# Weight rounding in a top-k attention kernel: the sign bit made on GpSimd, and the first piece loaded in halves

## The chip, the cores and the metric

The kernel runs on one core of a Trainium2 chip. The metric is the time of one execution on the device, in microseconds. Before the change it is 1476.7 us (median of three runs, 1475.35 to 1476.87); the profiled execution spans 1473.8 us.

## The reference

```python
# attention: q, k, v are (8, 8, 576, 64); top_k = 32
scores = scale * np.matmul(q, k.transpose(0, 1, 3, 2))
kth = np.partition(scores, -top_k, axis=-1)[..., -top_k:-top_k + 1]
mask = scores >= kth
scores = np.where(mask, scores, -1000000000.0)
scores = scores - np.max(scores, axis=-1, keepdims=True)
attn = np.exp(scores)
attn = attn / (np.sum(attn, axis=-1, keepdims=True) + 1e-09)
attn_out = np.matmul(attn, v)
# MLP on the heads laid side by side: x is (4608, 512)
h = x @ w_in                      # w_in (512, 2048)
g = np.maximum(0.01 * h, h)
out = (g @ w_out)                 # w_out (2048, 512)
```

The two weight matrices are float64 in the inputs (a float32 array divided or multiplied by a double scale), and the kernel gets them as 16-bit words, four to a number. Before it can use them it has to round each number to float32 on the chip. That rounding is all the change is about.

## The kernel before

The weights come in sixteen pieces of 128 x 1024 numbers, 1 MB each as 16-bit words. Word 3 of each number holds the sign, the exponent and the top four bits of the mantissa; word 2 and words 0 and 1 hold the rest. The piece is taken apart on three engines, TensorE adds three scaled parts up in PSUM, and VectorE multiplies the sum by a power of two with the sign in it.

```python
    raws = ctx.enter_context(tc.tile_pool(name="raws", bufs=3))
    work = ctx.enter_context(tc.tile_pool(name="work", bufs=2))
    ...
    def load_weights(n):
        ...
        raw_of[n] = raws.tile([P, WCH, 4], U16, name="raw")
        nc.sync.dma_start(raw_of[n].rearrange("p n w -> p (n w)"), weights[n])   # L102

    def round_weights(n):
        raw = raw_of.pop(n)
        dst = piece(n)
        mid = raw[:, :, 2]
        low = raw.rearrange("p n w -> p (n w)").bitcast(U32).rearrange("p (n w) -> p n w", w=2)[:, :, 0]
        top = raws.tile([P, WCH], U16, name="top", bufs=2)
        scale = raws.tile([P, WCH], U16, name="scale", bufs=2)
        parts = work.tile([P, 2 * NKC - 1, P], F32, name="wT", bufs=3)
        ...                                             # m_top, m_low lie in parts
        nc.gpsimd.tensor_copy(top, raw[:, :, 3])                                  # L119
        nc.scalar.activation(dst, mid, AF.Copy, bias=-7.0 - 2.0 ** -16, scale=2.0 ** -20)   # L120
        nc.scalar.activation(m_low, low, AF.Copy, bias=128.0, scale=2.0 ** -29)   # L122
        yield
        nc.vector.tensor_scalar(scale, top, 4, 0x7FF, ALU.logical_shift_right, ALU.bitwise_and)   # L124
        nc.vector.tensor_scalar(scale, scale, 1151.0, 896.0, ALU.min, ALU.max)    # L126
        if n < NPIECE - 2:
            nc.scalar.activation(scale, scale, AF.Copy, bias=-896.0 * 128, scale=128.0)   # L128
        else:
            nc.vector.tensor_scalar(scale, scale, 896.0, 128.0, ALU.subtract, ALU.mult)   # L130
        nc.vector.tensor_scalar(m_top, top, 0xF, 0x3F80, ALU.bitwise_and, ALU.bitwise_or)  # L131
        nc.vector.tensor_scalar(top, top, 0x8000, None, ALU.bitwise_and)          # L132
        ...                                             # pw: a PSUM tile
        for pw, c in sums:                              # two halves of 512
            at = slice(c, c + 512)
            nc.tensor.matmul(pw, ident_top, m_top[:, at].bitcast(BF16), start=True, stop=False)   # L142
            nc.tensor.matmul(pw, ident, dst[:, at], start=False, stop=False)      # L143
            nc.tensor.matmul(pw, ident_low, m_low[:, at], start=False, stop=True) # L144
        yield
        nc.vector.tensor_tensor(scale, scale, top, ALU.bitwise_or)                # L146
        for pw, c in ends:
            at = slice(c, c + pw.shape[-1])
            nc.vector.tensor_tensor(dst[:, at], pw, scale[:, at].bitcast(BF16), ALU.mult)   # L149
```

The three sections between the yields belong to three steps. At step n the kernel issues the first section of piece n, the second of piece n - 1 and the third of piece n - 2, and then the load of piece n + 3:

```python
        for n in range(3):
            load_weights(n)
        for n in range(NPIECE + 2):
            for i in (n, n - 1, n - 2) if AS_WORDS else ():
                if 0 <= i < NPIECE:
                    if i == n:
                        rounding[i] = round_weights(i)
                    next(rounding[i], None)
            load_weights(n + 3)
            ...                                         # first loads of q, k, v; first scores
```

After it comes the attention, in 144 units of 128 rows of two heads, with the MLP's matmuls laid between its steps. Of it the text needs the first instruction of the top-k search and the mask:

```python
    def top_k(u):
        ...
        for n, op in enumerate((ALU.max, ALU.min)):
            nc.vector.tensor_tensor(pairs[:, :, n, :], u.both[:, :, 0:HS], u.both[:, :, HS:S], op)   # L244
        ...                                             # rounds of max (L249) and match_replace (L252)

    def mask(u, i):
        if i == 0:
            ...
            nc.gpsimd.tensor_scalar(u.nbias, u.tops[:, :, 0, 0], -SCALE, None, ALU.mult)          # L260
        pen = work.tile([P, S], F32, name="pen", bufs=1)
        nc.gpsimd.tensor_scalar(pen, u.s[i], u.tops[:, i, ROUNDS - 1, 7:8], MASKED, ALU.is_lt, ALU.mult)   # L262
        nc.gpsimd.tensor_tensor(u.s[i], u.s[i], pen, ALU.add)                     # L263

    def transpose(u):
        ...
            split = work.tile([P, 2 * S], U16, name="split", bufs=2)
            nc.scalar.copy(split, pairs[:, :, h])                                 # L287
```

Of the kernel before, what the change touches and what calls it, by code (L numbers as in the profile page):

```python
# [10 lines left out]
U16 = mybir.dt.uint16  # L11
BF16 = mybir.dt.bfloat16
AF = mybir.ActivationFunctionType
ALU = mybir.AluOpType
# [5 lines left out]
def kernel(  # L20
# [13 lines left out]
    nc = tc.nc  # L34
    NPAIR, P, S = qT.shape
# [14 lines left out]
    WCH = 1024  # L50
# [11 lines left out]
    work = ctx.enter_context(tc.tile_pool(name="work", bufs=2))  # L62
# [22 lines left out]
    def piece(n):  # L85

        if n < NPIECE // 2:
            j, c = divmod(n, HP)
            return w_in[c][:, j * WCH:(j + 1) * WCH]
        f = 2 * (n - NPIECE // 2)  # L90
        return w_out[f // 4][:, f % 4:f % 4 + 2, :].rearrange("p g n -> p (g n)")

    raw_of = {}

    def load_weights(n):
        if n >= NPIECE:
            return
        if not AS_WORDS:
            nc.sync.dma_start(piece(n), weights[n])
            return  # L100
        raw_of[n] = raws.tile([P, WCH, 4], U16, name="raw")
        nc.sync.dma_start(raw_of[n].rearrange("p n w -> p (n w)"), weights[n])  # L102

    def round_weights(n):

# [10 lines that stand above are left out]
        parts = work.tile([P, 2 * NKC - 1, P], F32, name="wT", bufs=3)  # L116
        parts = parts.rearrange("p c n -> p (c n)").bitcast(U16)
        m_top, m_low = parts[:, 0:WCH], parts[:, WCH:2 * WCH].bitcast(BF16)
        nc.gpsimd.tensor_copy(top, raw[:, :, 3])  # L119
        nc.scalar.activation(dst, mid, AF.Copy, bias=-7.0 - 2.0 ** -16, scale=2.0 ** -20)  # L120

        nc.scalar.activation(m_low, low, AF.Copy, bias=128.0, scale=2.0 ** -29)  # L122
        yield
        nc.vector.tensor_scalar(scale, top, 4, 0x7FF, ALU.logical_shift_right, ALU.bitwise_and)  # L124

        nc.vector.tensor_scalar(scale, scale, 1151.0, 896.0, ALU.min, ALU.max)  # L126
        if n < NPIECE - 2:
            nc.scalar.activation(scale, scale, AF.Copy, bias=-896.0 * 128, scale=128.0)  # L128
        else:
            nc.vector.tensor_scalar(scale, scale, 896.0, 128.0, ALU.subtract, ALU.mult)  # L130
        nc.vector.tensor_scalar(m_top, top, 0xF, 0x3F80, ALU.bitwise_and, ALU.bitwise_or)  # L131
        nc.vector.tensor_scalar(top, top, 0x8000, None, ALU.bitwise_and)  # L132
        if n < NPIECE - 4 or n % 2 == 0:
            tag, bufs = ("wide", 2) if n < NPIECE - 4 else ("narrow", 1)
            pw = ps_sc.tile([P, 2, 512], F32, name=tag, bufs=bufs)
            sums = [(pw[:, h, :], h * 512) for h in range(2)]
            ends = [(pw.rearrange("p h n -> p (h n)"), 0)]
        else:
            ends = sums = [(ps_ml.tile([P, 512], F32, name="pw", tag="ml"), h * 512) for h in range(2)]
        for pw, c in sums:  # L140
            at = slice(c, c + 512)
            nc.tensor.matmul(pw, ident_top, m_top[:, at].bitcast(BF16), start=True, stop=False)  # L142
            nc.tensor.matmul(pw, ident, dst[:, at], start=False, stop=False)  # L143
            nc.tensor.matmul(pw, ident_low, m_low[:, at], start=False, stop=True)  # L144
        yield
        nc.vector.tensor_tensor(scale, scale, top, ALU.bitwise_or)  # L146
        for pw, c in ends:
            at = slice(c, c + pw.shape[-1])
            nc.vector.tensor_tensor(dst[:, at], pw, scale[:, at].bitcast(BF16), ALU.mult)  # L149
# [319 lines left out]
    with tc.manual_schedule():  # L469
# [11 lines left out]
        for n in range(3):  # L481
            load_weights(n)
        rounding = {}
# [7 lines that stand above are left out]
            if 6 <= n < 6 + HP:  # L491
                load_qk(n - 6)
            elif n == NPIECE - 3:
                first_scores(steps[0])
            elif n == NPIECE:
                first_scores(steps[1])
            if n == NPIECE - 1:
                load_v(0)
                load_v(1)
# [132 lines left out]
```

## Time and profile before

| | busy us | share of the span |
|---|---|---|
| TensorE matmuls (PE) | 1393.5 | 95% |
| VectorE (DVE) | 1328.3 | 90% |
| GpSimd (POOL) | 1097.7 | 74% |
| ScalarE (ACT) | 1096.2 | 74% |

| instruction of the rounding | engine | count | mean us |
|---|---|---|---|
| L119 copy of word 3 | GpSimd | 16 | 1.14 |
| L120, L122 conversions | ScalarE | 16 each | 1.15, 1.13 |
| L124, L126, L131, L132 on 16-bit words | VectorE | 16 each | 0.43, 0.43, 0.42, 0.43 |
| L146, both inputs 16-bit | VectorE | 16 | 0.68 |
| L149, 1024 numbers at once | VectorE | 14 | 1.22 |

In the lines of the profile, L is a line of the kernel, then come the engine, the operation, and what is written, an arrow, and what is read. In lists of groups, what follows the bar is the busy time of the group in us and the mean of one in ns, and behind the next bar the idle time before it with what ended it. In the timeline and in the chain the first number is the start in us from the beginning of the span and the second the duration; a line that ends in x2 is two instructions merged.

### The profile page before, as it was taken

The numbers are of one execution on the slowest core, as the hardware profiler recorded it, in microseconds if no ns is written. First come the engines' busy times: TensorE is split into PE (matmuls) and PEld (weight loads), VectorE is DVE, ScalarE is ACT, GpSimd is POOL, SyncE is SP. The second block draws the span as 40 slices with busy tenths as digits, with TensorE's granted clock in tenths as the row PEclk, the third lists the DMA queues.
The fourth block names the chain that finished last, engine by engine and source line by source line (L and its number), as shares of the span: only waits on it lengthen the run. The fifth ranks groups of instructions, "written<-read, shape, count | busy, mean of one in ns | idle before, by whom it ended". The sixth has DMA issues, their size and how long they took to land.

```text
span 1473.8 us, 24093 instructions
## 1 busy us (share of the span) xinstructions
PE 1393.5 (95%) x8057; PEld 927.6 (63%) x8059; DVE 1328.3 (90%) x3414; ACT 1096.2 (74%) x1979; POOL 1097.7 (74%) x742
## 2 busy tenths in 40 slices
PE   6716989999999999999999999999999999999998
PEld 2304547676766666666666666767676767676674
DVE  7999999999999999999999999999999999999600
ACT  8647887777787777777777777787877787877710
POOL 2278887888788888788878887888788888787700
PEclk9957999999999999999999999999999999999999
DMA  9724453655367554666466545565557555554510
GB/s 331 298 64 127 131 153 102 175 157 148 105 166 206 142 146 129 180 181 150 135 167 189 155 125 147 165 196 142 130 165 207 138 141 132 165 135 135 144 47 14
DMA packets 391421, 223.48 MB, mean 152 GB/s; under 512 B 336256, under 2 KB 336257, under 8 KB 389249
## 3 DMA queue, kind: packets, MB, share of 16 engines
q1 hardware_dynamic: 391296, 221.95, 53.6%
q8 instruction: 63, 1.03, 0.3%
q14 instruction: 62, 0.50, 0.1%
HBM read 46.14 MB, written 92.60 MB: 94 GB/s over the span
## 4 chain that ended last, share of the span: by engine, by line
PE 81%; DVE 14%; DMA 2%; ACT 2%; issue 1%; SPq 0%; POOL 0%; DVEq 0%; ACTq 0%
PE pz L390 31%; PE ph L378 30%; PE wide L327 10%; PE wide L214 6%; DVE tops L249 5%; DVE pairs L252 4%; PE narrow L214 3%; DVE pairs L244 1%; DMA wT<-apart 1%; ACT split L287 1%; DVE w_out L149 1%; DVE w_in L149 1%; DVE scale L146 1%; DVE scale L124 0%; ACT s_sb L278 0%
## 5 line engine op out<-in xcount | busy, mean ns | idle before, releaser
L262 POOL TENSOR_SCALAR pen<-s_sb,tops 128x576 f32<-128x576 f32 x288 | 638.3, 2216 | 207.7 <-DVE tops L249 120.2
L249 DVE MAX8 tops<-pairs 128x8 f32<-128x288 f32 (+1 forms) x1152 | 635.9, 591 | 0.0
L390 PE MATMUL pz<-w_out,gT 128*128 128x512 f32 x1152 | 508.4, 596 | 0.0
L378 PE MATMUL ph<-x,w_in 128*128 128x256 f32 x2176 | 481.1, 381 | 0.0
L252 DVE MATCH_REPLACE8 pairs<-tops,pairs 128x288 f32<-128x288 f32 (+1 forms) x864 | 460.1, 538 | 0.0
L378 PEld LDWEIGHTS ph<-x,w_in 128*128 128x128 f32 x2176 | 410.7, 190 | 77.1 <-issue 22.9
L263 POOL TENSOR_TENSOR s_sb<-s_sb,pen 128x576 f32<-128x576 f32 x288 | 406.9, 1413 | 24.0
L390 PEld LDWEIGHTS pz<-w_out,gT 128*128 128x128 f32 x1152 | 215.3, 190 | 265.8 <-issue 264.8
L287 ACT COPY split<-s_sb 128x1152 uint16<-128x1152 uint16 x282 | 309.1, 1145 | 0.0
L278 ACT ACTIVATE s_sb<-s_sb,rz 128x576 f32<-128x576 f32 x288 | 207.0, 769 | 38.7 <-DVE rz L275 38.5
L266 ACT ACTIVATE s_sb<-s_sb,nbias 128x576 f32<-128x576 f32 x288 | 221.0, 767 | 12.5 <-POOL s_sb L263 12.5
L244 DVE TENSOR_TENSOR pairs<-s_sb 128x576 f32<-128x576 f32 x288 | 213.6, 780 | 9.9
L327 PEld LDWEIGHTS wide<-wT,vt 128*64 128x64 f32 x3200 | 161.7, 139 | 67.4 <-ACT s_sb L221 26.5
L327 PE MATMUL wide<-wT,vt 128*64 128x128 f32 (+1 forms) x3200 | 179.9, 269 | 24.6 <-ACT s_sb L221 22.3
L384 ACT ACTIVATE gT<-ph 128x512 f32<-128x512 f32 x136 | 80.6, 593 | 80.0 <-PE ph L378 80.0
L341 ACT COPY x<-wide 128x128 f32<-128x128 f32 (+1 forms) x160 | 32.1, 260 | 131.5 <-PE wide L327 131.4
L221 ACT COPY s_sb<-wide 128x704 f32<-128x704 f32 x142 | 107.0, 754 | 23.2 <-PE wide L214 23.1
L214 PE MATMUL wide<-kt,qt 64*128 64x352 f32 (+1 forms) x392 | 75.8, 500 | 26.0 <-ACT s_sb L221 23.6
L221 ACT COPY s_sb<-narrow 128x448 f32<-128x448 f32 x142 | 68.7, 536 | 1.3 <-PE narrow L214 0.7
L397 ACT COPY o_sb<-pz 128x512 f32<-128x512 f32 x36 | 21.1, 585 | 59.4 <-PE pz L390 59.4
L275 DVE RECIPROCAL rz<-ze 128x2 f32<-128x2 f32 x144 | 22.3, 155 | 44.8 <-ACT ze L271 44.7
L252 DVE MATCH_VALUE_LOAD pairs<-tops,pairs 128x8 f32 x864 | 62.5, 72 | 0.0
(62 smaller groups left out, 622.7 us busy)
## 6 DMA issues: line engine op xcount, KB each, us to landing
apart<-split SPq DMA_DIRECT2D x282, 288.0 KB, 2.1
raw<-in_weights_dram SPq DMA_DIRECT2D x16, 1024.0 KB, 6.9
vt<-in_vk_dram SPq DMA_DIRECT2D x32, 320.0 KB, 3.4
out_dram<-o_sb SPq DMA_DIRECT2D x36, 256.0 KB, 2.0
qt<-in_qT_dram SPq DMA_DIRECT2D x20, 288.0 KB, 3.2
kt<-in_kT_dram SPq DMA_DIRECT2D x20, 288.0 KB, 3.6
raw<-in_qT_dram SPq DMA_DIRECT2D x12, 288.0 KB, 3.2
raw<-in_kT_dram SPq DMA_DIRECT2D x12, 288.0 KB, 3.7
```

What stands on the lines that cost most here:

```text
L214: nc.tensor.matmul(to[r0:r0 + u.rows, i, :], qt[d, u.q0:u.q0 + u.rows], kt[d, k0:k1], start=True, stop=True)
L244: nc.vector.tensor_tensor(pairs[:, :, n, :], u.both[:, :, 0:HS], u.both[:, :, HS:S], op)
L249: nc.vector.max(out=u.tops[:, i, r, :], in_=rest[i])
L252: nc.vector.match_replace(out=rest[i], in_to_replace=u.tops[:, i, r, :], in_values=rest[i], imm_value=LOWEST)
L262: nc.gpsimd.tensor_scalar(pen, u.s[i], u.tops[:, i, ROUNDS - 1, 7:8], MASKED, ALU.is_lt, ALU.mult)
L263: nc.gpsimd.tensor_tensor(u.s[i], u.s[i], pen, ALU.add)
L266: nc.scalar.activation(u.s[i], u.s[i], AF.Exp, bias=u.nbias[:, i:i + 1], scale=SCALE, accum_out=u.z[:, i:i + 1])
L278: nc.scalar.activation(u.s[i], u.s[i], AF.Copy, bias=0.0, scale=u.rz[:, i:i + 1])
L287: nc.scalar.copy(split, pairs[:, :, h])
L327: nc.tensor.matmul(po[side * D:(side + 1) * D, o, :], vt[:, c, side, :], u.wT[:, c + side * NKC if c + 1 < NKC else c, r:r + n], start=(c ...
L378: nc.tensor.matmul(ph[:, i, 0:n], w_in[c][:, f * P:(f + 1) * P], x[c][:, 0:n], start=(c == 0), stop=(c == HP - 1),)
L390: nc.tensor.matmul(pz[0:m, 0:DMODEL], gT[:, f, r0:r0 + m], w_out[f // 4][:, f % 4, :], start=(f == 0), stop=(f == NFC - 1),)
```

## The change

The sign bit was made on VectorE from the copied word (L132, in place). Now GpSimd makes it straight from the loaded words: a word of 32768 or more has its top bit set, so the comparison gives 1 or 0, and the multiplication by 32768 puts the bit where it belongs. This takes one instruction from VectorE and gives one to GpSimd. The sign has a buffer of its own now, which it shares by name with the later "split" tiles (two of them). Beside that, piece 0 is loaded and taken apart in two halves of 512 numbers, so that its first half can be worked on before the second has landed; L124 and L126 follow in halves for that piece, the rest works on the whole.

```diff
+    def parts_of(n):
+
+        step = WCH // 2 if n == 0 else WCH
+        return [slice(c, c + step) for c in range(0, WCH, step)]
...
-        nc.sync.dma_start(raw_of[n].rearrange("p n w -> p (n w)"), weights[n])
+        for at in parts_of(n):
+            nc.sync.dma_start(raw_of[n].rearrange("p n w -> p (n w)")[:, 4 * at.start:4 * at.stop],
+                              weights[n][:, 4 * at.start:4 * at.stop])
...
-        nc.gpsimd.tensor_copy(top, raw[:, :, 3])
-        nc.scalar.activation(dst, mid, AF.Copy, bias=-7.0 - 2.0 ** -16, scale=2.0 ** -20)
-
-        nc.scalar.activation(m_low, low, AF.Copy, bias=128.0, scale=2.0 ** -29)
+        sign = work.tile([P, 2 * S], U16, name="split", bufs=2)[:, 0:WCH]
+        for at in parts_of(n):
+            nc.gpsimd.tensor_copy(top[:, at], raw[:, at, 3])
+            nc.scalar.activation(dst[:, at], mid[:, at], AF.Copy, bias=-7.0 - 2.0 ** -16, scale=2.0 ** -20)
+
+            nc.scalar.activation(m_low[:, at], low[:, at], AF.Copy, bias=128.0, scale=2.0 ** -29)
+        nc.gpsimd.tensor_scalar(sign, raw[:, :, 3], 32768.0, 32768.0, ALU.is_ge, ALU.mult)
         yield
-        nc.vector.tensor_scalar(scale, top, 4, 0x7FF, ALU.logical_shift_right, ALU.bitwise_and)
-
-        nc.vector.tensor_scalar(scale, scale, 1151.0, 896.0, ALU.min, ALU.max)
+        for at in parts_of(n):
+            nc.vector.tensor_scalar(scale[:, at], top[:, at], 4, 0x7FF, ALU.logical_shift_right, ALU.bitwise_and)
+
+            nc.vector.tensor_scalar(scale[:, at], scale[:, at], 1151.0, 896.0, ALU.min, ALU.max)
...
-        nc.vector.tensor_scalar(top, top, 0x8000, None, ALU.bitwise_and)
...
-        nc.vector.tensor_tensor(scale, scale, top, ALU.bitwise_or)
+        nc.vector.tensor_tensor(scale, scale, sign, ALU.bitwise_or)
```

## The prediction

> **What bounds the kernel now.** I read the page first, then the window sums, the chain of waits inside the first 70 us, the waits by engine, and last the timeline of the engines that the change touches. In the page's slices TensorE stands at 9 tenths or more from about a tenth of the span on, and its chain is 81% TensorE. The change touches only the rounding of the sixteen weight pieces, and so the question is what that stage does to the start of the rest.
>
> The window sums of the first 70 us and of two later stretches:
>
> ```profile
> core 0: us, PE busy (x) PEld busy (x) DVE busy (x) ACT busy (x) POOL busy (x), PEclk, DMA share, GB/s
> 0.00:70.00 70.00, 48.40 (x150) 20.14 (x154) 57.69 (x104) 51.20 (x52) 18.97 (x22) 1.00 0.89 331
> 70.00:150.00 80.00, 32.14 (x180) 20.92 (x178) 79.34 (x207) 49.06 (x89) 62.32 (x42) 0.68 0.34 93
> 150.00:300.00 150.00, 144.22 (x939) 89.82 (x936) 145.92 (x385) 121.81 (x233) 124.52 (x83) 0.99 0.50 139
> ```
>
> After rounding, VectorE is full from 70 us (79.3 of 80), and TensorE is nearly full from 150 us; the first top-k search starts on VectorE right behind the last rounding instruction. There is no slack between the stages that could swallow a delay or hold back a gain: a rounding stage longer or shorter by D moves the end by about D.
>
> What sets the rounding stage's pace is VectorE. The chain, cut to one piece:
>
> ```profile
> 23.67 1.24 DVE w_in L149
> ...
> 25.00 0.44 DVE scale L124
> 25.43 0.02 issue
> 25.46 0.43 DVE scale L126
> 25.89 0.34 DVE wT L131
> 26.23 0.02 issue
> 26.25 0.43 DVE top L132
> 26.68 0.61 DVE scale L146
> ...
> 27.39 1.24 DVE w_in L149
> ```
>
> Every link is VectorE (the lines cut out are 0.1 us of issue); from 23.67 to 27.39 it is 3.72 us for one piece, and the other pieces repeat it. GpSimd copies one piece in 1.13 us and idles 2.6 us, waiting for VectorE's L146 to let go of a buffer. ScalarE has three passes of about 1.02 us from start to start, so 3.1 us. DMA moves 331 GB/s and is busy 89% of these 70 us, so it is not far behind. The last rounding instruction ends at 68.78 us.
>
> **What the Trainium skill says, and the trace.** (1) "GPSIMD Engine Reference", § 4.1 Engine selection: elementwise work with one input is roughly line-rate on GpSimd. The plain copy agrees (1024 elements in 1.13 us). The comparison with a multiplication doesn't: 576 elements take 2.22 us, and that row decides. (2) "VectorE: DVE Perf Modes", § What auto-detection actually checks: a one-source 16-bit instruction with both sides dense in SBUF runs four elements per cycle through both ports. L124, L126 and L131 are such: 1024 elements in 0.43 us, against 0.68 us for the two-source L146. (3) "SBUF — State Buffer", § Who interferes with whom: such an instruction shares a port pair with GpSimd, and whichever starts first holds it for the whole instruction; a VectorE instruction with two SBUF inputs contends with a GpSimd one that reads. The trace shows an exclusion, but a shorter one:
>
> ```profile
> 702.80 2.22 POOL L262 TENSOR_SCALAR pen<-s_sb,tops 128x576 f32<-128x576 f32 x1 [1.02 <-ACT s_sb L278]
> 703.37 1.45 DVE L244 TENSOR_TENSOR pairs<-s_sb 128x576 f32<-128x576 f32 x2
> ...
> 768.15 2.22 POOL L262 TENSOR_SCALAR pen<-s_sb,tops 128x576 f32<-128x576 f32 x1 [2.60 <-ACT gT L384]
> 768.37 1.80 DVE L244 TENSOR_TENSOR pairs<-s_sb 128x576 f32<-128x576 f32 x2
> ```
>
> The two VectorE instructions end 2.02 us after GpSimd's start in both cases (703.37 + 1.45 - 702.80 and 768.37 + 1.80 - 768.15), although they began 0.57 and 0.22 us after it. Undisturbed they take 1.41 us together. So they were held until 2.02 - 1.41 = 0.61 us after the comparison began, and then ran at full speed beside its remaining 1.61 us: VectorE's second read waits for GpSimd's reading and not for the whole instruction. What GpSimd's writing does to a four-per-cycle VectorE instruction, which also needs the second write port, the trace can't say: no two of them overlap, except once in the other order:
>
> ```profile
> 8.15 0.43 DVE L132 TENSOR_SCALAR top<-top 128x1024 uint16<-128x1024 uint16 x1
> 8.21 1.35 POOL L119 COPY top<-raw 128x1024 uint16<-128x1024 uint16 x1 [1.35 <-DMA raw<-in_weights_dram]
> ```
>
> There the copy took 1.35 us instead of 1.13: GpSimd was held by VectorE.
>
> **The change part by part.** *Removed:* L132, one VectorE instruction per piece; in the chain 0.43 us with 0.02 us of issue, and L146 then follows L131 directly. VectorE alone would go at 3.72 - 0.44 = 3.28 us per piece. Over sixteen pieces that is 7.0 us, the most the removal can be worth; ScalarE's 3.1 us and the DMA's 89% leave room for only part of it.
>
> *Added on GpSimd:* per piece one tensor_scalar over 1024 elements, comparison and multiplication. The rows to size it, of the page and of the groups of the first 190 us:
>
> ```profile
> L262 POOL TENSOR_SCALAR pen<-s_sb,tops 128x576 f32<-128x576 f32 x288 | 638.3, 2216 | 207.7 <-DVE tops L249 120.2
> ...
> L260 POOL TENSOR_SCALAR nbias<-tops 128x2 f32<-128x2 f32 x13 | 3.0, 233 | 9.6 <-DVE tops L249 8.5
> ```
>
> Two elements cost 233 ns, 576 cost 2216: (2216 - 233) / 574 = 3.45 ns an element. For 1024: 0.233 + 1022 x 0.00345 = 3.76 us. I chose this row over the copy's 1.13 us because it is the same form, a comparison then a multiplication; it differs in type (f32 here, 16-bit words there) and in its first operand (one value per partition, not a constant), and either could shift the size. The strided read is the copy's own, and that one is fast.
>
> With gaps of 0.09 us between GpSimd's instructions (seen between its L263 and L260), a piece costs GpSimd 1.13 + 3.76 + 2 x 0.09 = 5.07 us. That is over VectorE's 3.28 and over the old pace of 3.72. So GpSimd becomes the bound, and the release of the raw buffers comes later too.
>
> *Without any exclusion* (case A): the first piece's second half lands near 5.7 us, its copy ends near 6.4, its comparison at 6.4 + 0.09 + 3.76 = 10.25, and the sixteenth at 10.25 + 15 x 5.07 = 86.3. Then L146 (0.7) and the last L149 pair (1.3): 88.4 against 68.8. D = +19.6 us, so 1496.
>
> *With the exclusion:* when a copy ends, VectorE's L124 starts 0.03 us later (in the timeline, copy end 6.86, L124 at 6.89), before GpSimd's next instruction with its 0.09. The comparison then waits for one (0.46 us) up to three (L124, L126, L131: 1.25 us) VectorE instructions in each piece. Case B: 5.53 to 6.32 us a piece, or sixteen times 0.46 to 1.25 on top of case A, 7 to 20 us: 1504 to 1516. If the comparison holds the pair for all of its 3.76 us (case C), L124, L126, L131 and L146 all stand in one line with GpSimd's two, as comparison n also needs the sign buffer that L146 of piece n - 2 frees: 5.07 + 1.9 = 6.97 us a piece, D = 19.6 + 16 x 1.9 = 50, so 1527.
>
> *Moved:* the first piece in halves. The first half should land one to two us earlier, and L124 starts its half earlier. But piece 1 lands at about 8.2 us as before, and in the old trace VectorE already stood idle 1.01 us before L124 of piece 1. So I give the halves nothing: what they bring forward ends in the next wait. The extra instructions of one piece are under 1 us.
>
> **The rivals.** First: the comparison runs at the copy's speed, some 1.1 to 1.3 us. Then GpSimd needs 2.5 us a piece, VectorE stays the bound at 3.28 us, and 3 to 7 us are gained: 1470 to 1474. For it speak the copy's row and the skill's line-rate; against it the same form at 3.45 ns an element. One chance in ten. Second: the comparison is slow, but the port is no matter (case A, 1496); the two pairs ending at 2.02 us speak for a short hold. Third: case C, a full lock, for which the skill speaks; the trace shows it released early for reads only. Fourth: 16-bit words make the comparison slower than 3.76 us, by conversion both ways; each further us is 16 us, and at 4.5 us case A alone reaches 1508. A fifth, that later stages absorb the delay, I reject: VectorE is at 99% right after rounding.
>
> **Range and chances.** Weights: fast comparison 0.10 (near 1472), A 0.15 (1496), B short 0.20 (1504), B long 0.20 (1516), C 0.35 (1527). The median lies near 1514 us. I predict 1514, with 1484 to 1532 to hold it eight times in ten. The 2% lines are 1447 and 1506: faster by 2% would need 30 us where at most 7 are to be had, so 0.01. Above 1506 lie B long, C and part of B short, with a slower comparison: 0.62. Within 2%: 0.37.
>
> **What would show each step right or wrong.** GpSimd's new row: about 3.8 us mean, sixteen of them; its busy time up by some 60 us, to about 1158. VectorE's L132 gone, L124 waiting for GpSimd's copy in every piece, and L124 or L126 stretched over 0.43 us if the pair is locked. From one L149 to the next 5.1 to 7.0 us instead of 3.72, and the last one near 88 to 119 us instead of 68.8. From there on the trace should be the old one shifted. A new row of about 1.2 us, or a last L149 before 68 us, would make the prediction wrong in its main step; a late L149 with an unmoved end would make the one-to-one shift wrong.

## The result, and the profile after

The changed kernel takes 1492.2 us (median of four, 1492.0 to 1492.4) against 1476.8 us: 1.0107 times the time before, 95% interval 1.0089 to 1.0124, so 15.4 us more. The prediction was 1514 us, a loss of 37 us, with a range of 1484 to 1532 us.

In the listings of the changed kernel the lines have moved: the copy is L128 (it was L119), the comparison L132, and VectorE's L124, L126, L131, L146 and L149 are L135, L137, L142, L156 and L159.

The window sums of the first two of the prediction's three stretches:

```profile
core 0: us, PE busy (x) PEld busy (x) DVE busy (x) ACT busy (x) POOL busy (x), PEclk, DMA share, GB/s
0.00:70.00 70.00, 44.99 (x112) 17.30 (x113) 50.83 (x69) 44.80 (x45) 64.91 (x35) 0.90 0.74 264
70.00:150.00 80.00, 28.39 (x154) 17.27 (x155) 78.10 (x191) 44.78 (x77) 60.84 (x39) 0.67 0.39 125
```

GpSimd went from 19.0 to 64.9 us in the first 70: it is busy from the first piece to the last. VectorE and the transfers went down. The chain of waits over two pieces of the same stage:

```profile
20.25 0.12 POOL top L128
20.37 0.95 issue
21.32 2.82 POOL split L132
24.14 0.81 issue
24.95 0.13 POOL top L128
25.08 0.96 issue
26.04 2.82 POOL split L132
```

VectorE is gone from it; all is GpSimd's copy and comparison (the chain books a part of each as issue, as it does where one instruction starts before the end of the one in front). From 21.32 to 26.04 it is 4.72 us a piece, against 3.72 before. The groups of the first 90 us:

```profile
L132 POOL TENSOR_SCALAR split<-raw 128x1024 uint16<-128x1024 uint16 x16 | 59.6, 3726 | 0.1
L128 POOL COPY top<-raw 128x1024 uint16<-128x1024 uint16 x15 | 17.2, 1145 | 0.0
...
L135 DVE TENSOR_SCALAR scale<-top 128x1024 uint16<-128x1024 uint16 x15 | 19.6, 1309 | 11.8 <-POOL top L128 11.6
L142 DVE TENSOR_SCALAR wT<-top 128x1024 uint16<-128x1024 uint16 x16 | 6.7, 419 | 0.0
```

The comparison takes 3.73 us, and GpSimd has no idle time before it. L135 (the old L124) went from 0.43 to 1.31 us; L142 is unchanged. Last, VectorE's timeline where the top-k search begins, in the kernel before and then after the change, here with the last rounding instructions:

```profile
68.69 1.41 DVE L244 TENSOR_TENSOR pairs<-s_sb 128x576 f32<-128x576 f32 x2
```

```profile
83.14 1.29 DVE L159 TENSOR_TENSOR w_out<-pw,scale 128x512 f32<-128x512 f32 x2
84.34 1.42 DVE L254 TENSOR_TENSOR pairs<-s_sb 128x576 f32<-128x576 f32 x2
```

The search starts at 84.34 us; before the change it started at 68.69. The stage is 15.65 us longer, the whole kernel 15.4.

### The profile page after: what moved, and what is told of

Read it like the earlier page. It is cut to its first block, busy times and chain, and to the rows that moved or that the text cites. A ratio compares the mean times of both kernels' runs of the same rounds, so it can differ in the third digit from the quotient of the medians.

```text
span 1490.4 us, 24115 instructions
## 1 busy us (share of the span) xinstructions
PE 1401.7 (94%) x8059; PEld 929.6 (62%) x8059; DVE 1335.6 (90%) x3400; ACT 1097.0 (74%) x1981; POOL 1155.0 (77%) x759
## 3 DMA queue, kind: packets, MB, share of 16 engines
q8 instruction: 63, 1.03, 0.3%
## 4 chain that ended last, share of the span: by engine, by line
PE 84%; DVE 10%; POOL 3%; issue 2%; DMA 1%; ACT 1%; SPq 0%; DVEq 0%; POOLq 0%; ACTq 0%
PE pz L400 32%; PE ph L388 32%; PE wide L337 10%; PE wide L224 6%; DVE tops L259 4%; PE narrow L224 3%; DVE pairs L262 3%; POOL split L132 2%; DVE pairs L254 1%; DMA wT<-apart 1%; POOL top L128 1%; DVE scale L135 1%; DMA raw<-in_weights_dram 0%; DVE scale L156 0%; ACT split L297 0%
```

## The experiments

Two theories could make 15 us out of this. Theory 1: GpSimd's two instructions, one behind the other, are the pace, and VectorE's waits lie beside them. Theory 2: VectorE's path itself got longer, since L135 is stretched by 0.88 us in sixteen pieces, 14 us, which is very near the loss. Against these 14 us stand the 7 us of the removed instruction, so by its own sum theory 2 explains half of the loss. The first four runs shared one series of the kernel before (median 1476.0 us), the last three another (1476.5).

**e1_sign_only.** The halves are taken out of the change.

```diff
-        step = WCH // 2 if n == 0 else WCH
+        step = WCH
```

Expected:

> The change without its halves: the comparison on GpSimd, piece 0 loaded and taken apart whole. Theory 1 (GpSimd's two instructions, 1.07 + 3.64 us from start to start, set the pace of 4.71 us a piece): the same pace; piece 0's copy should start near 5.75 us and end at 6.86 instead of 6.99, so the comparison of piece 0 starts some 0.2 us earlier: 1491.5 to 1492.3 us. If the halves were a gain as meant, it is 1493 us or more.

Measured: 1491.6 us, ratio 1.0104 (1.0090 to 1.0118). The comparison of piece 0 starts at 6.76 us instead of 7.08, and the top-k search 0.30 us earlier (84.04). The intervals of this run and of the change overlap; the traces say that the halves bring nothing here, the times don't contradict.

**e2_halves_only.** The kernel before with the halves.

```diff
-        nc.sync.dma_start(raw_of[n].rearrange("p n w -> p (n w)"), weights[n])
+        for at in parts_of(n):      # two halves for n == 0, else the whole
+            nc.sync.dma_start(raw_of[n].rearrange("p n w -> p (n w)")[:, 4 * at.start:4 * at.stop],
+                              weights[n][:, 4 * at.start:4 * at.stop])
     ...                             # copy, L120, L122, L124, L126 in the same halves; L132 kept
```

> The halves alone, with the sign bit still made on VectorE as before. The four loads at the start share the transfer engines, and with the change piece 1 was first used at 8.99 us instead of 8.18 us. VectorE sets the pace from piece 1 on, so this should cost about what piece 1 comes later: +0.3 to +0.9 us, 1477.1 to 1477.7 us. If the halves help as meant: 1475 to 1476 us.

Measured: 1477.8 us, ratio 1.0009 (1.0003 to 1.0016): a small loss. GpSimd's timeline of this run shows when the pieces can be used:

```profile
4.86 0.64 POOL L127 COPY top<-raw 128x512 uint16<-128x512 uint16 x1 [3.58 <-DMA raw<-in_weights_dram]
6.38 0.64 POOL L127 COPY top<-raw 128x512 uint16<-128x512 uint16 x1 [0.87 <-DMA raw<-in_weights_dram]
9.09 1.11 POOL L127 COPY top<-raw 128x1024 uint16<-128x1024 uint16 x1 [2.08 <-DMA raw<-in_weights_dram]
```

The first half is there at 4.86 us, 0.9 us before the whole piece came in the kernel before (5.75). But the second half comes at 6.38 and piece 1 at 9.09 instead of 8.21. The top-k search starts at 69.22 instead of 68.69, 0.5 us later; the median is 1.8 us up, more than this trace explains.

**e4_comparison_added.** The kernel before, with the comparison added on GpSimd and its result used by nobody. VectorE does all its old work.

```diff
         nc.scalar.activation(m_low, low, AF.Copy, bias=128.0, scale=2.0 ** -29)
+        sign = work.tile([P, 2 * S], U16, name="split", bufs=2)[:, 0:WCH]
+        nc.gpsimd.tensor_scalar(sign, raw[:, :, 3], 32768.0, 32768.0, ALU.is_ge, ALU.mult)
```

> The kernel before with the comparison added on GpSimd and its result used by nobody; VectorE keeps all its instructions. Theory 1 (GpSimd's 4.71 us a piece are the bound and VectorE has slack beside it): as with the change, 1491 to 1494 us. Theory 2 (the loss is VectorE's own path: 16 stretches of L124 by 0.88 us, 14 us, against which 16 x 0.44 = 7 us of removed work stand): 7 us more than with the change, about 1499 us.

Measured: 1494.1 us, ratio 1.0121 (1.0107 to 1.0135). Theory 1 holds, theory 2 asked for 1499. From piece 1 to piece 14 GpSimd has no idle time and takes 4.71 us a piece, as in e1_sign_only, so VectorE's removed instruction is worth nothing while GpSimd sets the pace. That the run is 2.5 us over e1_sign_only comes from the last two pieces, in which VectorE also does L130, and so L132 comes late enough to be held. GpSimd's and VectorE's timelines there:

```profile
73.02 3.73 POOL L124 TENSOR_SCALAR split<-raw 128x1024 uint16<-128x1024 uint16 x1
77.69 1.10 POOL L119 COPY top<-raw 128x1024 uint16<-128x1024 uint16 x1 [0.94 <-DVE scale L148]
```

```profile
73.14 1.30 DVE L126 TENSOR_SCALAR scale<-top 128x1024 uint16<-128x1024 uint16 x1 [0.24 <-POOL top L119]
74.48 0.43 DVE L128 TENSOR_SCALAR scale<-scale 128x1024 uint16<-128x1024 uint16 x1
74.94 0.43 DVE L132 TENSOR_SCALAR scale<-scale 128x1024 uint16<-128x1024 uint16 x1
75.28 0.42 DVE L133 TENSOR_SCALAR wT<-top 128x1024 uint16<-128x1024 uint16 x1
75.74 1.30 DVE L134 TENSOR_SCALAR top<-top 128x1024 uint16<-128x1024 uint16 x1
```

Here L126 to L134 are the kernel's L124, L126, L130, L131 and L132. The first is held until 0.99 us after the comparison's start (73.14 + 1.30 - 0.43 - 73.02); this is called the first stretch below. The next three run in their usual 0.43 us beside the comparison. The fifth, which starts 2.72 us after the comparison, is held again, until 3.59 us after it (the second stretch); nothing else ran on GpSimd then, as its next copy starts only at 77.69. L148 comes later by that, and GpSimd's next copy waits 0.94 us for it. e8_two_more tests this second hold.

**e3_copy_for_comparison.** As e1_sign_only, with a plain copy in the comparison's place. It leaves out the taking of the sign bit.

```diff
-        nc.gpsimd.tensor_scalar(sign, raw[:, :, 3], 32768.0, 32768.0, ALU.is_ge, ALU.mult)
+        nc.gpsimd.tensor_copy(sign, raw[:, :, 3])
```

> The change without halves, and a plain copy of the word in place of the comparison (it leaves out the taking of the sign bit; the word goes into the or whole). GpSimd then needs 2 x 1.07 = 2.2 us a piece and is not the bound; it still reads as many elements. Theory 1 with the hold for the reading: VectorE's 3.28 us plus 0.5 to 0.9 us for which one of its instructions waits for GpSimd's reads, 3.8 to 4.2 us a piece: 1477 to 1484 us. Without any effect of the hold: 3.28 to 3.4 us a piece, 1470 to 1472 us.

Measured: 1481.6 us, ratio 1.0035 (1.0023 to 1.0046), still slower than before although GpSimd is idle 1.8 us in each piece. GpSimd's and then VectorE's timeline of one piece:

```profile
45.40 1.14 POOL L132 COPY split<-raw 128x1024 uint16<-128x1024 uint16 x1 [1.82 <-DVE scale L156]
46.46 1.12 POOL L128 COPY top<-raw 128x1024 uint16<-128x1024 uint16 x1
49.40 1.14 POOL L132 COPY split<-raw 128x1024 uint16<-128x1024 uint16 x1 [1.81 <-DVE scale L156]
```

```profile
45.37 1.23 DVE L159 TENSOR_TENSOR w_out<-wide,scale 128x1024 f32<-128x1024 f32 x1
46.70 1.17 DVE L135 TENSOR_SCALAR scale<-top 128x1024 uint16<-128x1024 uint16 x1
47.90 0.43 DVE L137 TENSOR_SCALAR scale<-scale 128x1024 uint16<-128x1024 uint16 x1
48.24 0.42 DVE L142 TENSOR_SCALAR wT<-top 128x1024 uint16<-128x1024 uint16 x1
48.58 0.69 DVE L156 TENSOR_TENSOR scale<-scale,split 128x1024 uint16<-128x1024 uint16 x1
```

The piece takes 4.00 us (45.40 to 49.40). The first copy hides beside L159, which reads PSUM and only one operand from SBUF; the second runs into L135 and stretches it by 0.74 us. This is theory 2's mechanism, and it is real where VectorE is the bound: the hold (0.74) is more than the instruction saved (0.44). In the kernel before, GpSimd's only copy stood beside that instruction, which took its usual 1.22 us:

```profile
23.63 1.13 POOL L119 COPY top<-raw 128x1024 uint16<-128x1024 uint16 x1 [2.59 <-DVE scale L146]
```

```profile
23.67 1.22 DVE L149 TENSOR_TENSOR w_in<-wide,scale 128x1024 f32<-128x1024 f32 x1
```

**e5_one_operation.** As e1_sign_only, without the multiplication; it leaves out putting the bit into its place.

```diff
-        nc.gpsimd.tensor_scalar(sign, raw[:, :, 3], 32768.0, 32768.0, ALU.is_ge, ALU.mult)
+        nc.gpsimd.tensor_scalar(sign, raw[:, :, 3], 32768.0, None, ALU.is_ge)
```

> The change without halves, and the comparison without the multiplication (it leaves out putting the 1 into the top bit). If each of the two operations costs its share of the 3.45 ns an element, GpSimd's instruction falls to about 2.0 us and its two together to 3.1 us a piece; GpSimd is then no longer the bound, and VectorE's 3.28 us plus the wait for GpSimd's reads set the pace, about 4.0 us: near 1481 us. If the second operation is free, the instruction stays at 3.7 us and the time at 1491 to 1492 us.

Measured: 1484.7 us, ratio 1.0056 (1.0043 to 1.0070), which neither expectation had. Its row among the groups of the first 105 us:

```profile
L132 POOL TENSOR_SCALAR split<-raw 128x1024 uint16<-128x1024 uint16 x16 | 48.7, 3044 | 1.1 <-DVE scale L156 1.0
```

The mean of 3.04 us hides two values. GpSimd's and VectorE's timelines of one of the pieces 1 to 13, and of piece 14:

```profile
19.21 3.07 POOL L132 TENSOR_SCALAR split<-raw 128x1024 uint16<-128x1024 uint16 x1
...
64.43 2.83 POOL L132 TENSOR_SCALAR split<-raw 128x1024 uint16<-128x1024 uint16 x1
```

```profile
20.97 0.42 DVE L142 TENSOR_SCALAR wT<-top 128x1024 uint16<-128x1024 uint16 x1
...
66.31 1.24 DVE L141 TENSOR_SCALAR scale<-scale 128x1024 uint16<-128x1024 uint16 x1
```

In pieces 1 to 13 L142 starts about 1.76 us after the comparison and runs freely, and the comparison takes 3.06 to 3.09 us. In the last two a VectorE instruction that starts 1.88 or 1.80 us after it is held until about 2.69 us, and the comparison takes 2.83. So here VectorE delays GpSimd, by 0.24 us a piece; undisturbed, the comparison alone is 2.83 us, 2.5 copies, and the multiplication adds nearly 0.9 (2.83 against 3.7).

From piece 1 to piece 14 GpSimd has no idle time, and a piece takes 4.11 us against 4.71 in e1_sign_only. The chain view names VectorE there, but VectorE has room: L135 is let go 0.96 us after the comparison's start whether it comes 0.10 us after it (39.86 against 39.76) or 0.54 (44.40 against 43.86). So GpSimd still sets the pace, as theory 1 has it. The comparison of piece 14 starts 8.4 us earlier than in e1_sign_only (64.43 against 72.86); in the last two pieces the holds on VectorE give 1.7 us of this back. Since VectorE's 3.28 us and a hold of 0.85 also make 4.1 us a piece, this run alone would not tell the theories apart; e4_comparison_added does.

**e7_fused_on_vector.** Another way to save the instruction: on VectorE alone.

```diff
-        nc.vector.tensor_scalar(top, top, 0x8000, None, ALU.bitwise_and)
     ...
-        nc.vector.tensor_tensor(scale, scale, top, ALU.bitwise_or)
+        nc.vector.scalar_tensor_tensor(scale, top, 0x8000, scale, ALU.bitwise_and, ALU.bitwise_or)
```

> The kernel before, with L132 and L146 fused into one VectorE instruction (and with a constant, then or with a tensor); nothing is added on GpSimd. If the fused form goes at two elements per cycle like L146 (0.68 us), VectorE needs 3.28 us a piece: 1470 to 1473 us. If at one element per cycle ([...]1.22 us, in place of 0.44 + 0.61): 0.17 us a piece more than before, about 1478.5 us.

Measured: 1479.1 us, ratio 1.0018 (1.0011 to 1.0026). The fused instruction takes 1.22 us, the slow one of the two cases expected, and is longer than the two that it replaces (0.44 + 0.61 us in the chain).

**e8_two_more.** As e1_sign_only, with L142 done three times.

```diff
         nc.vector.tensor_scalar(m_top, top, 0xF, 0x3F80, ALU.bitwise_and, ALU.bitwise_or)
+        nc.vector.tensor_scalar(m_top, top, 0xF, 0x3F80, ALU.bitwise_and, ALU.bitwise_or)
+        nc.vector.tensor_scalar(m_top, top, 0xF, 0x3F80, ALU.bitwise_and, ALU.bitwise_or)
```

> The change without halves, and L142, the masking of the mantissa bits, done three times in place of once (the same result each time). In the run with the comparison added, two VectorE instructions that started 2.67 and 2.71 us after the comparison were held until about 3.56 us after it, which a hold for the reading alone doesn't give. If GpSimd holds the pair a second time near its end, the third L142, which would start some 2.5 to 2.9 us after the comparison, waits in every piece until 3.5 us: its mean is about 1.0 us or more and VectorE's pace near 5.5 us, about 1503 us. If the hold is the reading alone: VectorE 3.28 + 0.88 + 0.68 = 4.84 us a piece, 1493 to 1495 us.

Measured: 1510.3 us, ratio 1.0231 (1.0216 to 1.0247). GpSimd's and VectorE's timelines of one piece (L142, L143 and L144 are the three):

```profile
40.71 3.85 POOL L132 TENSOR_SCALAR split<-raw 128x1024 uint16<-128x1024 uint16 x1 [0.71 <-DVE scale L158]
44.51 1.32 POOL L128 COPY top<-raw 128x1024 uint16<-128x1024 uint16 x1
```

```profile
42.79 0.42 DVE L142 TENSOR_SCALAR wT<-top 128x1024 uint16<-128x1024 uint16 x1
43.24 0.43 DVE L143 TENSOR_SCALAR wT<-top 128x1024 uint16<-128x1024 uint16 x1
43.70 1.13 DVE L144 TENSOR_SCALAR wT<-top 128x1024 uint16<-128x1024 uint16 x1
44.76 1.63 DVE L158 TENSOR_TENSOR scale<-scale,split 128x1024 uint16<-128x1024 uint16 x1
```

L143 begins 2.53 us after the comparison and runs freely. L144 begins 2.99 us after it and takes 1.13: it gets through at about 44.83 - 0.42 = 44.41, just before the comparison ends at 44.56. Most pieces look like this; the mean of L144 is 1.06 us. So the second hold is real. The time went past the 1503 us expected because the next copy then holds L158 as well, for 0.9 us, and the comparison, which waits 0.71 us for L158 in most pieces, itself became 0.15 us longer: L143 was running when it needed the pair again. L135 is not held in most pieces here (0.43 us), as it starts 1.27 us after the comparison, when the first stretch is over.

## Why the prediction was wrong

By its own steps:

- *VectorE sets the pace before the change, and the stage's length passes one to one to the end:* right. By run, what the start of the top-k search moved and what the median moved: the change 15.6 and 15.4 us, e1_sign_only 15.4 and 15.6, e4_comparison_added 17.9 and 18.1, e5_one_operation 8.6 and 8.2, e8_two_more 33.6 and 33.8. The small ones are less clear: e2_halves_only 0.5 and 1.8, e7_fused_on_vector 3.0 and 2.6, e3_copy_for_comparison 4.1 and 5.5 (its trace is of its fastest execution, 1479.7). Single executions of the kernel before lie between 1475.0 and 1479.1 us.
- *The comparison takes 3.76 us, from the mask's row at 3.45 ns an element:* right, 3.73 measured; type, step and constant operand together made no difference that shows. The Trainium skill's "roughly line-rate" for one input ("GPSIMD Engine Reference", § 4.1) holds for the copy and not for this.
- *GpSimd becomes the bound, at 5.07 us a piece:* right in kind, 0.36 us too much. I added 0.09 us between two instructions, taken from the attention. Here the next one starts before the end of the one in front, by 0.02 to 0.14 us, so the pace is 4.71. In the piece shown below that is 0.27 us of the difference (2 x 0.09, and overlaps of 0.04 and 0.05); the comparison, 3.68 us there, accounts for the rest. Over fifteen pieces this is 5 us, and case A comes down from 1496 to 1491. What is left is two small misses: the comparison of piece 0 ended at 10.86 us and not 10.25, and what follows the last comparison took 2.9 us and not 2.1.
- *The exclusion adds 0.46 to 1.9 us to each piece (cases B and C, 75% of the weight):* **this is the step that failed.** It rested on VectorE's L124 starting before the comparison, as it was 0.03 us behind the copy against GpSimd's 0.09. The timelines of one piece after the change, GpSimd and then VectorE:

```profile
15.53 1.13 POOL L128 COPY top<-raw 128x1024 uint16<-128x1024 uint16 x1
16.62 3.68 POOL L132 TENSOR_SCALAR split<-raw 128x1024 uint16<-128x1024 uint16 x1
20.25 1.10 POOL L128 COPY top<-raw 128x1024 uint16<-128x1024 uint16 x1
```

```profile
16.69 1.29 DVE L135 TENSOR_SCALAR scale<-top 128x1024 uint16<-128x1024 uint16 x1 [0.69 <-POOL top L128]
18.02 0.43 DVE L137 TENSOR_SCALAR scale<-scale 128x1024 uint16<-128x1024 uint16 x1
18.36 0.42 DVE L142 TENSOR_SCALAR wT<-top 128x1024 uint16<-128x1024 uint16 x1
```

  The comparison starts at 16.62, L135 at 16.69. VectorE did come 0.03 us behind the copy's end, as assumed, but GpSimd came 0.04 us before it. So GpSimd is first, and it is VectorE that waits. It waits until 0.93 us after the comparison's start (16.69 + 1.29 - 0.43 = 17.55, less 16.62) and no longer, and it has the time: it stands idle 0.69 us before L135 anyway. GpSimd loses nothing. The prediction's own two pairs had this order, with GpSimd first, its 2.22 us unchanged and VectorE held; the sum then put the cost on GpSimd.

  Only for piece 0 is the order the one that I assumed. GpSimd and VectorE there, in e1_sign_only, without the halves:

```profile
6.76 3.91 POOL L132 TENSOR_SCALAR split<-raw 128x1024 uint16<-128x1024 uint16 x1
```

```profile
6.70 0.43 DVE L135 TENSOR_SCALAR scale<-top 128x1024 uint16<-128x1024 uint16 x1 [5.02 <-POOL top L128]
```

  The comparison took 3.91 us: 0.22 us more than the usual 3.69, and not the 0.46 of the one instruction in front of it. The copy behind L132 in the prediction lost as much (1.35 against 1.13). So the term of the sum should have been near nothing, and case A, which had a weight of 0.15, was the one that came. It could have been more: in e5_one_operation VectorE did lengthen the comparison, by 0.24 us in most pieces, as L142 was running there when the comparison needed the pair a second time. In the change L142 ends before that (2.16 us after the comparison's start in the piece shown first).
- *A full lock (case C):* wrong. The Trainium skill, "SBUF — State Buffer", § Who interferes with whom, has the first one holding the pair for its whole instruction; in these runs GpSimd's comparison holds it for its first 0.93 to 1.03 us and for some 0.9 us near its end, and in e4_comparison_added three VectorE instructions of the four-per-cycle kind go through in between at full speed.
- *The halves give nothing:* right for the gain. But piece 1 did not land at 8.2 us as before: its copy could start only at 9.09 in e2_halves_only. In the kernel before the halves cost a little (1.0003 to 1.0016).

No version tried beats the kernel before. VectorE has one stretch in each piece, the 1.3 us of L149, in which GpSimd's copy didn't hold it, and the copy fills that already; a second GpSimd pass would then hold VectorE somewhere else. That is argued from e3_copy_for_comparison; a version with the comparison in some of the pieces only was not tried.

## What to carry to other kernels

An instruction moved to an engine that is idle costs what it takes there, so read the cost from a row of the same form on that engine (here 3.7 us for 0.43) and compare it with the idle time per piece (here 2.6 us), not with the engine's share of the span. Fitting in is not enough: in e3_copy_for_comparison a pass of 1.14 us fitted, and its hold on VectorE cost more than the instruction saved. Before weighing an exclusion between two engines, ask which of the two starts first and whether the one that waits has slack: a hold on an engine off the path costs nothing, and the same hold costs its full length where that engine is the bound. And look at what is loaded behind a load that is split: here the halves brought the first data 0.9 us earlier and piece 1 0.9 us later.

## What the runs showed of the hardware

A GpSimd instruction over 1024 16-bit words held VectorE's four-per-cycle instructions for its first 0.93 to 1.03 us (0.94 to 0.98 us for a copy in e3_copy_for_comparison). The comparison with its multiplication held them a second time: in e4_comparison_added and e8_two_more those that started 2.67 to 2.72 us after it got through at 3.54 to 3.59 of its 3.7 us. One that started just before that ran on, and the comparison took longer instead (e8_two_more: started 2.49 us after it, 3.80 us; 2.53, 3.85; 2.61, 3.91; where the one to come then started at 2.67 and was held, 3.69). A VectorE instruction with two SBUF inputs behaved otherwise: in e4_comparison_added L148 started 2.53 to 2.58 us after the comparison and ran across the second stretch in its usual 0.68 us, and the comparison kept its 3.67 to 3.72 us. In the first stretch such a one is held (the two pairs of the prediction, and L158 behind the copy in e8_two_more). Reading in the first stretch and writing in the second would explain both; that is inferred and not shown.

A comparison on GpSimd cost 2.5 times a copy of the same words where nothing disturbed it (2.83 against 1.13 us), and a multiplication behind it nearly 0.9 us more. Two GpSimd instructions that don't wait for one another overlapped by 0.02 to 0.14 us in pieces 1 to 15; in piece 0 the comparison started 0.09 us behind the copy, and why is open. A VectorE instruction with a constant and two 16-bit tensors took 1.22 us for 1024 (e7_fused_on_vector), where one with two tensors alone takes 0.68.
